# Block-sparse attention and a gated feed-forward layer on one core: loads, row numbers, queues and low parts of the first jobs

## The chip, the cores and the metric

One core of a Trainium2 chip. The metric is the device time of one execution in microseconds; the comparison is by the median of the runs.

## The reference, cut to what matters

```python
B, H, S, D = 4, 8, 768, 64            # block = 32, 24 blocks
scores = (q @ k.T) / sqrt(D)          # masked: neighbours, first and last block, 3 sampled blocks of each row of blocks
attn = softmax(scores); x = (attn @ v) as (B*S, H*D) = (3072, 512)
h = x @ w_in                          # 512 -> 2048, weights float64
g = h * tanh(log1p(exp(h)))
out = g @ w_out                       # 2048 -> 512
```

## The kernel before, in words

Every float32 operand of a product is cut into a high and a low float16 part, and each product is three matmuls (high-high, high-low, low-high). A low part is the scaled value less its high part; in the kernel before it is made by VectorE or GpSimd.

**Attention.** A batch is 13 jobs: blocks 0 and 23 are dense (all 768 keys), the other 22 blocks of queries go in pairs, called here the two halves of a job. A half has 256 keys: three neighbours, two global blocks, three sampled ones. `gather_k` (L537) copies the sampled keys inside SBUF on GpSimd (L544). `gather_v` (L551) fetches values from the DRAM copy `vd`, which `store_v` (L500) writes: one DMA for the neighbours (L560) and three for the sampled blocks (L567), all by SyncE's queue, each of the three after a load of its row number into a register (L528, from the table `offv`); of three numbers two stay in registers for later batches. There are two buffers of gathered keys and two of gathered values (L306); `globals_v` (L516) puts the global blocks there. A job then runs: scores `s` on TensorE (L604), maximum on VectorE (L647), exponentials on ScalarE (L670), transposes `t` on TensorE (L690), high part `ph` on ScalarE (L693), low part `pl` on VectorE (L697), product with values into `obank` (L719, for early jobs one half at a time), division `xs` on VectorE (L741), transposes `tx` (L748), high part `xh` (ScalarE, L766), low part `xl` (VectorE, L769). The PSUM ring `t` has two buffers and each is held from L690 until `pl` is made.

**Values, batch 0.** `load` (L368) puts q, k and v into the ring `raw` of six buffers. Tiles in `APART` (L498) are scaled in place on ScalarE or GpSimd (L466, L468), their high part is on ScalarE (L477) and their low part on GpSimd (L483); others take ScalarE (L448) and VectorE (L452).

**Weights.** They arrive as float64: 8 pieces of w_in (1 MB, ring `wr` of three) and 16 of w_out (0.5 MB, ring `raw`), loaded by SyncE's queue (L785). VectorE puts float32 together in three steps each (L793, L796, L799); TensorE, VectorE and ScalarE find a scale, and GpSimd makes the low parts (L857, L896).

**Feed-forward.** 12 tiles of 256 tokens. `moe_h` (L924) makes h (L935) and `moe_g` (L951) the gate in the ring `us` (L958 to L968) and two parts `g` (L976, L979, ring of four); `moe_y` (L982) multiplies by w_out (L994), one tile behind. Tile 0 needs the results of jobs 0 to 4.

**Order.** No loop sets the order. Every step is a task with an engine, an assumed duration, its inputs and outputs and a key; `Plan.emit` (L85) places tasks one after another by the assumed times, and a smaller key goes earlier. What is emitted is a fixed program for each engine. `START` (L1136) holds back a job's scores against other work of TensorE, and idle stretches of the plan between 14 and 200 us are filled with matmuls on zeros (L1173).

Of the kernel before, what the change touches and what calls it, by code (L numbers as in the profile page):

```python
# [26 lines left out]
             xs=2, hs=3, us=3, g=4, ys=1, kt=1, q=2, ssk=2, ssv=2, ssq=2, sck=2, scv=2, scq=2, iv=2, ns=3, ws=2,  # L27
# [13 lines left out]
class Plan:  # L41
# [43 lines left out]
    def emit(self, pace, fill):  # L85
# [6 lines left out]
        free, ready, dma = {}, {}, 0.0  # L92
# [10 lines left out]
        while todo:  # L103
# [35 lines left out]
            if port and free.get("POOL", 0.0) > start:  # L139
                t.dur *= 1.3  # L140
            end = start + t.dur + (pace(t, None) or 0.0)
            free[t.eng] = end
            if t.kind and t.kind[0] == "dma":

                dma = max(dma, end) + t.kind[1]
                t.end = max(dma, end + t.lat)
            else:
                t.end = end + t.lat
# [19 lines left out]
def attn_mish_kernel(ctx: ExitStack, tc: tile.TileContext, qT, kT, v, sampled, blocks, w_in, w_out, out):  # L168
# [45 lines left out]
    wo = const.tile([P, NFC, 2, DM], F16, name="wo")  # L214
    iv_i = const.tile([P, NFP], F32, name="iv_i")
    iv_o = const.tile([P, 1], F32, name="iv_o")
    sc_o = const.tile([P, 1], F32, name="sc_o")
    gsc = const.tile([P, NFP], F32, name="gsc")
    gmx = const.tile([P, 1], F32, name="gmx")
    iv_x = const.tile([P, B], F32, name="iv_x")  # L220
    iv_k = const.tile([P, B], F32, name="iv_k")
    gox = const.tile([P, 1], F32, name="gox")
# [19 lines left out]
    def which(new):  # L242
        room = new(sb, "raw", ("z",), [P, RAW])
# [47 lines left out]
    zeros = const.tile([P, NZ], F16, name="zeros")  # L291
    nc.gpsimd.memset(zeros, 0.0)
# [13 lines left out]
    NKG = NVG = 2  # L306
# [37 lines left out]
    def root_pe(key, ss, apart):  # L344

        n = ss.shape[-1]
        tp = new(ps["t"], "t", key, [P, n if apart else 1])
# [15 lines left out]
    def add_root(key, ss, fn, r, after, w, new, cls, n=1, apart=False):  # L363

        add("PE", 0.3 * n, lambda: root_pe(key, ss(), apart), r=r, w=[key], new=[("t", key)], key=cls - 2, lat=0.3)
        add("DVE", 0.6, fn, r=[key, *after], w=w, new=new, key=cls)

    def load(b, what, js, ring="raw", after=()):  # L368
# [3 lines left out]
        def fn():  # L372
            for j, key in zip(js, keys):
                raw = new(sb, ring, key, [P, RAW])[:, 0:4 * TT]
# [30 lines left out]
    def scales(b, what, j, cls):  # L405
# [4 lines left out]
        def fn():  # L410
# [5 lines left out]
            if q:  # L416

                ns = new(sb, "ns", ("ns", b, j), [P, 2])
                for n, sign in enumerate((1.0, -1.0)):
# [4 lines left out]
                 [(f"sc{what}", key)] + ([("ns", ("ns", b, j))] if q else []), cls, 1 if q or not b else NTT)  # L424
# [73 lines left out]
    APART = {("v", 0, 0), ("v", 0, 1), ("v", 0, 2), ("q", 0, 1), ("q", 0, 2), ("k", 1, 0), ("k", 1, 1), ("k", 1, 2)}  # L498
# [25 lines left out]
    def block_at(eng, name, table, k, hi):  # L524
# [4 lines left out]
        if k % NR < 2:  # L529
            regs[name, k] = j  # L530
        return j

# [4 lines left out]
    def gather_k(su):  # L537
# [3 lines left out]
        def fn():  # L541
            for k, c0 in slots(su):
                j = block_at(nc.gpsimd, "k", offk, k, S - BS)
                nc.gpsimd.tensor_copy(out=kgs[n][:, :, c0:c0 + BS], in_=tl["kt", b][:, :, ds(j, BS)])  # L544
# [676 lines left out]
```

## Time and profile before

| what | us |
|---|---|
| runs | 796.12, 790.94, 795.52; median 795.52 |
| the profiled execution | 792.27, its span 790.5 |
| TensorE busy in the span | 740.3 (94%) |
| VectorE, ScalarE, GpSimd busy | 523.3, 534.0, 350.2 |

The profile is of one execution. Busy time of TensorE counts filler matmuls, and matmuls are pipelined, so busy is not the same as full. A stretch table gives each engine's busy time between two moments; the queue of SyncE (SPq) shows DMA issues, not transfers.

### The profile page before, as it was taken

The page shows a single profiled execution, that of the slowest core. Times are in us where ns is not written, and L with a number is a line of the kernel's source. Part 1 is how long each engine was busy: PE and PEld are TensorE (multiplying, and loading weights), DVE is VectorE, ACT ScalarE, POOL GpSimd, SP SyncE. Part 2 cuts the span into 40 slices and gives each one's busy share as a digit, 9 for nine tenths or more (in the row PEclk, how much of TensorE's full clock was granted, in tenths as well). Part 3 has the DMA queues.
Part 4 walks back from the last instruction along what each step waited for, and adds up shares of the span by engine and source line. Part 5 has one row for each costly group of instructions (what it writes and reads, how often), then busy time and mean ns, then how long its engine had stood idle before and what let it go on. Part 6 is the DMA issues. An engine that isn't in the chain of part 4 may idle for free.

```text
span 790.5 us, 30717 instructions
## 1 busy us (share of the span) xinstructions
PE 740.3 (94%) x12857; PEld 528.6 (67%) x12857; DVE 523.3 (66%) x914; ACT 534.0 (68%) x831; POOL 350.2 (44%) x413
## 2 busy tenths in 40 slices
PE   5757769999999999999999999999999999999997
PEld 4646658766577667776777676667677676666653
DVE  5998888689977755669566766786867553323240
ACT  2565246788787857887877787867877774555550
POOL 2499442589953424425433643345444431303031
PEclk9958889999999999999999999999999999999999
DMA  8855867612424356326424454253343243000000
GB/s 285 283 170 160 246 192 210 171 54 64 128 95 133 87 154 195 88 89 191 117 68 116 135 166 132 68 172 103 82 115 105 76 134 84 15 14 14 14 14 27
DMA packets 56974, 94.25 MB, mean 119 GB/s; under 512 B 8067, under 2 KB 20356, under 8 KB 56836
## 3 DMA queue, kind: packets, MB, share of 16 engines
q1 hardware_dynamic: 56640, 92.03, 38.5%
q8 instruction: 101, 1.65, 0.9%
q14 instruction: 37, 0.30, 0.1%
q10 hardware_dynamic: 196, 0.27, 0.1%
HBM read 79.32 MB, written 12.95 MB: 117 GB/s over the span
## 4 chain that ended last, share of the span: by engine, by line
PE 75%; DVE 14%; DMA 4%; ACT 2%; issue 2%; POOL 2%; SPq 1%; POOLq 0%; ACTq 0%; DVEq 0%
PE y L994 28%; PE h L935 27%; PE t L690 6%; PE obank L719 5%; PE s L604 5%; PE obank L1173 2%; DVE wi L796 2%; DVE pl L697 1%; PE tx L748 1%; DVE mx L647 1%; DVE wi L799 1%; DVE hs L968 1%; DMA vg<-vd 1%; DVE us L962 1%; DVE q L452 1%
## 5 line engine op out<-in xcount | busy, mean ns | idle before, releaser
L935 PE MATMUL h<-xh,wi 128*128 128x256 f16 x1536 | 283.6, 273 | 0.0
L994 PE MATMUL y<-wo,g 128*128 128x512 f16 x1152 | 276.7, 379 | 3.0 <-POOL wo L896 1.4
L935 PEld LDWEIGHTS <-wi 128*128 128x128 f16 x2304 | 223.9, 98 | 51.0 <-issue 2.4
L935 PE MATMUL h<-xl,wi 128*128 128x256 f16 x768 | 210.0, 273 | 0.7 <-issue 0.7
L979 POOL TENSOR_TENSOR g<-hs,g 128x1024 f16<-128x1024 f32 x48 | 105.9, 2206 | 187.8 <-DVE g L976 158.1
L994 PEld LDWEIGHTS <-g 128*128 128x128 f16 x1152 | 110.4, 98 | 105.5 <-issue 6.2
L544 POOL COPY kg<-kt 128x256 f16 x264 | 118.3, 488 | 110.1 <-PE s L604 103.7
L944 ACT ACTIVATE hs<-h,gsc 128x512 f32<-128x512 f32 x96 | 65.5, 684 | 73.1 <-PE h L935 71.7
L670 ACT ACTIVATE pt<-s,nb,ns 128x256 f32<-128x256 f32 (+1 forms) x208 | 106.4, 582 | 6.6 <-DVE nb L660 3.4
L697 DVE SCALAR_TENSOR_TENSOR pl<-t,ph 128x512 f16<-128x512 f32 x112 | 75.6, 683 | 39.8 <-ACT ph L693 39.6
L693 ACT ACTIVATE ph<-t 128x512 f16<-128x512 f32 x112 | 65.5, 594 | 50.6 <-PE t L690 34.6
L968 DVE SCALAR_TENSOR_TENSOR hs<-us,hs 128x1024 f32<-128x1024 f32 x48 | 65.5, 1364 | 33.2 <-ACT us L967 33.2
L690 PE MATMUL t<-ident,pt 128*128 128x128 f32 x448 | 72.9, 287 | 6.8 <-DVE pl L697 4.8
L964 POOL TENSOR_TENSOR us<-us 128x1024 f32<-128x1024 f32 x21 | 40.9, 1949 | 74.6 <-DVE us L962 68.9
L962 DVE TENSOR_SCALAR us<-us 128x1024 f32<-128x1024 f32 x48 | 41.9, 872 | 39.4 <-ACT us L958 39.2
L719 PEld LDWEIGHTS <-ph 128*32 128x32 f16 x3584 | 49.0, 95 | 27.3 <-issue 18.8
L690 PEld LDWEIGHTS t<-ident,pt 128*128 128x128 f32 x448 | 52.9, 145 | 17.7 <-DVE pl L697 6.8
L647 DVE TENSOR_REDUCE mx<-s 128x4 f32<-128x1024 f32 x44 | 53.3, 1211 | 4.2 <-PE s L604 4.2
L958 ACT ACTIVATE us<-hs,hsc 128x1024 f32<-128x1024 f32 x48 | 55.2, 1151 | 1.0
L719 PE MATMUL obank<-vg,ph 128*32 128x65 f16 (+1 forms) x3072 | 49.2, 197 | 6.5 <-DMA vg<-vd 4.3
L966 ACT ACTIVATE us<-us 128x1024 f32<-128x1024 f32 x48 | 50.7, 1055 | 4.7 <-POOL us L964 4.1
L967 ACT ACTIVATE us<-us 128x1024 f32<-128x1024 f32 x48 | 50.7, 1056 | 0.7
(193 smaller groups left out, 945.9 us busy)
## 6 DMA issues: line engine op xcount, KB each, us to landing
vg<-vd SPq DMA_DIRECT2D x304, 65.0 KB, 2.4
vg<-vd SPq DMA_DIRECT2D x80, 195.0 KB, 2.9
wr<-in_moe_w_in_dram SPq DMA_DIRECT2D x8, 1024.0 KB, 6.7
wor<-in_moe_w_out_dram SPq DMA_DIRECT2D x16, 512.0 KB, 4.5
vd<-v SPq DMA_DIRECT2D x12, 520.0 KB, 3.6
raw_k<-in_k_dram SPq DMA_DIRECT2D x12, 512.0 KB, 4.9
raw_q<-in_q_dram SPq DMA_DIRECT2D x12, 512.0 KB, 4.2
raw_v<-in_v_dram SPq DMA_DIRECT2D x12, 512.0 KB, 6.0
```

Of the source, the lines that this page charges most:

```text
L544: nc.gpsimd.tensor_copy(out=kgs[n][:, :, c0:c0 + BS], in_=tl["kt", b][:, :, ds(j, BS)])
L647: nc.vector.tensor_reduce(out=mx.rearrange("p g w -> p (g w)"), in_=tl[ks].rearrange("p g (w k) -> p (g w) k", k=KT), axis=AX.X, op=ALU.max)
L670: ex = lambda o, x, g, w: nc.scalar.activation(out=o, in_=x, func=AF.Exp, bias=nb[:, g, w:w + 1], scale=tl["ns", b, sus[w]["qb"] // TB][:, ...
L690: nc.tensor.transpose(t[:, k, g], src, ident)
L693: nc.scalar.activation(out=new(sb, "ph", ("ph", i, j), [P, 2, 2, P], F16), in_=tl["t", i, j], func=AF.Copy, scale=PSC)
L697: nc.vector.scalar_tensor_tensor(out=new(sb, "pl", ("pl", i, j), [P, 2, 2, P], F16), in0=tl["t", i, j], scalar=PSC, in1=tl["ph", i, j], op ...
L719: nc.tensor.matmul(o[cs, w, g, 0:v1 - v0], p[:, k, g, cs], vt[:, k, 2 * c + g, v0:v1], start=j == 0 and g == 0 and k == 0 and n == 0, stop ...
L935: nc.tensor.matmul(h[:, f2].rearrange("p (s q) -> p s q", q=BS), wi[:, fp, w, cc, fs], x[:, :, cc], start=f2 == 0 and k == 0, stop=f2 == 1 ...
L944: nc.scalar.activation(out=tl[kq][:, 2 * (fp % 2):2 * (fp % 2) + 2], in_=tl[kh], func=AF.Copy, scale=gsc[:, fp:fp + 1])
L968: add("DVE", 1.32, lambda: nc.vector.scalar_tensor_tensor(out=hs(), in0=us(), scalar=-0.5, in1=hs(), op0=ALU.add, op1=ALU.mult), r=[ku], w ...
L979: add("POOL", 2.3, lambda: nc.gpsimd.tensor_tensor(out=g()[:, 1], in0=hs(), in1=g()[:, 0], op=ALU.subtract), r=[kq, ("gh", b, t, k)], w=[kg])
L994: nc.tensor.matmul(tl[ky], tl["g", b, t, k][:, g, f, q], wo[:, fc, w], start=fc == 0 and n == 0, stop=fc == NFC - 1 and n == 2)
```

## The change

The values of batch 0, and the first tile of q, are loaded into buffers of the rings `us` and `hs` instead of `raw`, and their parts are made by ScalarE and VectorE. The row numbers that stay in registers are loaded for batch 0 by SyncE as tasks of their own (`registers`). All loads of weights are issued by ScalarE's queue. There are three buffers of gathered values; the ring `us` has two instead of three. For jobs 0 to 6 (`APL`) and for the first piece of w_in (`LPE`) the low part is made so: TensorE adds the negative of the high part into the PSUM bank that holds the value (a matmul with a negative identity), and ScalarE reads the bank. The gathered keys of jobs 0 to 6 may be copied by ScalarE. Job 12 takes the neighbours of the keys out of the batch's own tile, in matmuls of their own, instead of copying them (`WHOLE`; job 13 is dense), and job 11's product with values is one task (`SPLIT`). The planner counts the DMA time of each queue apart and takes GpSimd 15% slower beside VectorE. The roots of batch 0's k and first q use the PSUM ring `y`. Keys, `START` and the moments of batch 1's loads differ.

```diff
-             ... us=3, g=4, ...
+             ... us=2, g=4, ...
...
             if port and free.get("POOL", 0.0) > start:
                 t.dur *= 1.3
+            elif t.eng == "POOL" and free.get("DVE", 0.0) > start:
+                t.dur *= 1.15
...
+    neg = const.tile([P, 2, P], F16, name="neg")
+    nc.vector.tensor_scalar(out=neg[:, 0], in0=ident, scalar1=-1.0, scalar2=None, op0=ALU.mult)
+    nc.vector.tensor_scalar(out=neg[:, 1], in0=ident, scalar1=-1.0 / PSC, scalar2=None, op0=ALU.mult)
...
-    NKG = NVG = 2
+    NKG, NVG = 2, 3
...
-    APART = {("v", 0, 0), ("v", 0, 1), ("v", 0, 2), ("q", 0, 1), ...
+    APART = {("q", 0, 1), ...
...
-        if k % NR < 2:
+        if stays(name, k):
             regs[name, k] = j
+    def stays(name, k):
+        return k % NR < 2
+    def registers(su):
+        for r in range(NR):
+            k = su["qb"] * NR + r
+            if stays("v", k):
+                add("SP", 0.75, lambda k=k: block_at(nc.sync, "v", offv, k, S), r=["off"], w=[("reg", k)], key=99)
...
+                if eng == "ACT":
+                    j = nc.scalar.value_load(offk[0:1, k:k + 1], min_val=0, max_val=S - BS)
+                    nc.scalar.activation(out=dst, in_=tl["kt", b][:, :, ds(j, BS)], func=AF.Copy)
...
+        add("POOL", 0.53 * NR, lambda: fn("POOL"), r=KT3(b) + ["off"], w=[("kg", n)], use=[("kt", b)], key=-3,
+            also=[("ACT", 0.55 * NR, lambda: fn("ACT"))] if su["early"] else ())
...
-    WHOLE = 12
-    SPLIT = 12
+    WHOLE = 14
+    SPLIT = 11
+    APL = 7
...
+        def td_fn(j):
+            nc.tensor.matmul(tl["t", i, j].rearrange("p k g q -> p (k g q)"), neg[:, 1],
+                             tl["ph", i, j].rearrange("p k g q -> p (k g q)"), start=False, stop=True,
+                             skip_group_check=True)
+        def plf_fn(j):
+            nc.scalar.activation(out=new(sb, "pl", ("pl", i, j), [P, 2, 2, P], F16), in_=tl["t", i, j], func=AF.Copy,
+                                 scale=PSC)
...
+            if i < APL:
+                add("PE", 0.23, lambda j=j: td_fn(j), r=[("ph", i, j)], w=[kj], key=-3, lat=0.25, kind=("T", i))
+                add("ACT", 0.62, lambda j=j: plf_fn(j), r=[kj], w=[("pl", i, j)], new=[("pl", ("pl", i, j))],
+                    key=-2.5)
+                continue
...
+            run(lambda x, hi, lo: nc.tensor.matmul(x, neg[:, 0], hi, start=False, stop=True, skip_group_check=True))
+            run(lambda x, hi, lo: nc.scalar.activation(out=lo, in_=x, func=AF.Copy))
...
+        if i < APL:
+            add("PE", 0.15, xd_fn, r=[("xhw", i)], w=[("tx", i)], use=kx, key=-3, lat=0.25, kind=("X", i))
+            add("ACT", 0.4, xlf_fn, r=[("tx", i)], w=[("xw", i)], use=kx, key=-1.5)
+        else:
+            add("DVE", 0.45, xl_fn, r=[("tx", i), ("xhw", i)], w=[("xw", i)], use=kx, key=-1.5)
...
-        nc.sync.dma_start(out=raw.rearrange(...) if len(w.shape) == 3 else raw, in_=w)
+        nc.scalar.dma_start(out=raw.rearrange(...) if len(w.shape) == 3 else raw, in_=w)
...
-            add("SP", 0.5, lambda: load_w(pools["w"], raw, "wr", src, None), w=[raw], new=[("wr", raw)], key=-2,
-                lat=2.0, kind=("dma", 4.4))
+            add("ACT", 0.45, lambda: load_w(pools["w"], raw, "wr", src, None), r=after, w=[raw], new=[("wr", raw)],
+                key=-9, lat=2.0, kind=("dma", 4.4))
...
+        if k >= LPE:
+            add("POOL", 2.1, lambda: nc.gpsimd.tensor_tensor(out=lo, in0=tl[kt], in1=hi, op=ALU.subtract),
+                r=[kt, ("wih", k)], w=[("wi", k)], key=cls)
+            return
+        for n in range(2):
...
+                nc.tensor.matmul(d, ident, tl[kt][:, cs], start=True, stop=False)
+                nc.tensor.matmul(d, neg[:, 0], hi[:, cs], start=False, stop=True)
+            add("ACT", 0.62, lambda kd=kd, cs=cs: nc.scalar.activation(out=lo[:, cs], in_=tl[kd], func=AF.Copy),
+                r=[kd], w=[("wl", k, n)], key=cls)
...
-        add("SP", 0.5, lambda: load_w(sb, raw, "raw", ...), r=after, w=[raw, ("wo", fc)], ..., key=0, ...)
+        add("ACT", 0.45, lambda: load_w(sb, raw, "raw", ...), r=after, w=[raw, ("wo", fc)], ..., key=-5, ...)
...
-    AT0, ATV, ATW = -16.0, -28.0, 2.0
+    LPE = 1
+    AT0, ATV, ATW = -15.0, -19.0, 1.0
...
-    load(0, "q", [0])
+    load(0, "q", [0], "hs")
     for j in T3:
-        load(0, "v", [j])
+        load(0, "v", [j], "us" if j < 2 else "hs")
...
+    for job in jobs[0:JB]:
+        for su in job["sus"]:
+            if not job["dense"]:
+                registers(su)
...
-            PREP = (6, 4, 3) if b else (8, 1, 8)
+            PREP = (6, 4, 3) if b else (8, 2, 7)
...
-            LOADO, ATO, ATP = [("dec", 6)], -1.0, -4.0
+            LOADO, ATO, ATP = [("dec", 6)], -1.0, -15.0
...
-    RES, START = 155.0, [0, 51, 57, 72, 69, 48, 81, 72, 9, 0, 0, 0, 0, 0]
+    RES, START = 155.0, [0, 66, 57, 72, 72, 57, 99, 72, 15, 12, 9, 24, 6, 18]
```

## Rows read from the trace of the kernel before

**Rows 1.** The page's first line, and its row of TensorE's busy tenths in 40 equal slices of the span.
```profile
span 790.5 us, 30717 instructions
...
PE   5757769999999999999999999999999999999997
```
**Rows 2.** Busy time of each engine in four stretches (us from the span's start, length, then busy us and number of instructions of PE, PEld, DVE, ACT, POOL, then the granted clock, the DMA engines' share and GB/s).
```profile
0.00:122.00 122.00, 83.34 (x1944) 67.25 (x1945) 103.72 (x196) 56.09 (x90) 72.10 (x88) 0.85 0.70 224
122.00:200.00 78.00, 73.27 (x1413) 57.44 (x1411) 64.94 (x104) 64.81 (x106) 52.51 (x41) 0.98 0.44 126
200.00:790.50 590.50, 583.67 (x9504) 403.92 (x9502) 354.67 (x616) 413.12 (x636) 225.54 (x286) 1.00 0.33 97
...
10.00:122.00 112.00, 79.62 (x1918) 64.31 (x1917) 99.90 (x175) 54.81 (x89) 70.14 (x79) 0.83 0.69 219
```
**Rows 3.** The first matmul of the feed-forward part in order of time, the row of all matmuls with w_out (duration min/median/max in ns, first and last start in us), the filler matmuls of the first 122 us by line and shape (busy us, mean ns), and the matmuls of L935 alone in two stretches (busy us and number on PE, then on PEld).
```profile
121.60 0.42 PE L935 MATMUL h<-xh,wi 128*128 128x256 f16 x1
...
L994 PE MATMUL y<-wo,g x1152: 376/379/391, 157.9 to 785.9; 128*128 128x512 f16 x192
...
L1173 PE MATMUL obank<-zeros 128*128 128x240 f16 x231 | 34.2, 302 | 5.7 <-DVE xs L741 5.4 <-issue 0.3
...
122.00:157.90 35.90, 24.30 (x192) 18.30 (x189) 0.95 0.66 183
157.90:200.00 42.10, 21.46 (x182) 17.29 (x180) 1.00 0.26 77
```
**Rows 4.** SyncE's queue in order of time (start us, length of the merged piece us, what).
```profile
13.39 0.91 SPq L381 DMA_DIRECT2D raw_v<-in_v_dram  x1
...
37.53 2.92 SPq L501 DMA_DIRECT2D vd<-v  x2
...
56.73 0.38 SPq L501 DMA_DIRECT2D vd<-v  x1
57.17 5.79 SPq L519 DMA_DIRECT2D vg<-vd  x4
63.01 0.63 SPq L560 DMA_DIRECT2D vg<-vd  x1
...
69.76 2.57 SPq L567 DMA_DIRECT2D vg<-vd  x3
```
**Rows 5.** The same queue by line, 60 to 122 us for the gathers: issue time min/median/max in ns, first and last start; then the time from issue to landing of L567, and the issues of w_out.
```profile
L560 SPq DMA_DIRECT2D vg<-vd x12: 323/380/632, 63.0 to 120.8; - x12
...
DMA to landing us min/median/max: 1.8/4.1/6.5
...
L785 SPq DMA_DIRECT2D wor<-in_moe_w_out_dram x16: 328/382/1040, 72.9 to 120.3; - x16
```
**Rows 6.** VectorE in order of time: the products xs of jobs 1 and 4.
```profile
79.33 0.42 DVE L741 TENSOR_TENSOR xs<-obank,r 128x256 f32<-128x256 f32 x1
...
110.71 0.42 DVE L741 TENSOR_TENSOR xs<-obank,r 128x256 f32<-128x256 f32 x1
```
**Rows 7.** VectorE, 0 to 122 us, by line and shape (number | busy us, mean ns | idle before), then single lines with min/median/max in ns.
```profile
L796 DVE SCALAR_TENSOR_TENSOR wi<-wr,wi 128x1024 int32<-128x1024 int32 x8 | 15.3, 1915 | 0.0
L799 DVE SCALAR_TENSOR_TENSOR wi<-wr,wi 128x1024 int32<-128x1024 int32 x8 | 11.8, 1474 | 0.0
L697 DVE SCALAR_TENSOR_TENSOR pl<-t,ph 128x512 f16<-128x512 f32 x16 | 10.8, 682 | 3.8 <-ACT ph L693 3.8
L796 DVE SCALAR_TENSOR_TENSOR wo<-wor,wo 128x512 int32<-128x512 int32 x11 | 10.6, 963 | 0.0
...
L452 DVE SCALAR_TENSOR_TENSOR q<-raw_q,sc_q,q 128x1024 f16<-128x1024 f32 x1 | 1.3, 1277 | 0.0
...
L769 DVE TENSOR_TENSOR xl<-tx,xh x6: 273/350/417, 62.9 to 116.8; 128x128 f16<-128x128 f32 x3, 128x256 f16<-128x256 f32 x3
...
L796 DVE SCALAR_TENSOR_TENSOR wi<-wr,wi x8: 1212/1314/3149, 22.3 to 68.0; 128x1024 int32<-128x1024 int32 x8
L799 DVE SCALAR_TENSOR_TENSOR wi<-wr,wi x8: 1210/1223/2939, 24.0 to 71.6; 128x1024 int32<-128x1024 int32 x8
...
L796 DVE SCALAR_TENSOR_TENSOR wo<-wor,wo x16: 678/683/2499, 80.3 to 134.6; 128x512 int32<-128x512 int32 x16
```
**Rows 8.** GpSimd, 0 to 122 us, by line and shape.
```profile
L544 POOL COPY kg<-kt 128x256 f16 x54 | 28.0, 548 | 15.1 <-PE s L604 11.1 <-POOL kg L544 2.2 <-issue 1.1
L857 POOL TENSOR_TENSOR wi<-wt_i,wi 128x1024 f16<-128x1024 f32 x8 | 19.7, 2472 | 4.0 <-ACT wi L854 3.9
L483 POOL TENSOR_TENSOR v<-raw_v,v 128x1024 f16<-128x1024 f32 x3 | 7.6, 2557 | 0.0
...
L468 POOL TENSOR_SCALAR raw_v<-raw_v,sc_v 128x1024 f32<-128x1024 f32 x1 | 2.1, 2074 | 11.2 <-DVE gram_wi L340 11.2
```
**Rows 9.** ScalarE, 0 to 122 us, by line and shape.
```profile
L693 ACT ACTIVATE ph<-t 128x512 f16<-128x512 f32 x17 | 10.1, 596 | 25.9 <-PE obank L719 13.5 <-PE t L690 12.3
...
L466 ACT ACTIVATE raw_v<-raw_v,sc_v 128x1024 f32<-128x1024 f32 x2 | 2.3, 1144 | 2.5 <-DVE sc_v L231 2.5
...
L766 ACT ACTIVATE xh<-tx 128x256 f16<-128x256 f32 x3 | 1.2, 386 | 2.1 <-PE tx L748 2.1
```
**Rows 10.** One of VectorE's lines of the feed-forward part over the whole run (min/median/max ns).
```profile
L968 DVE SCALAR_TENSOR_TENSOR hs<-us,hs x48: 1207/1224/3152, 141.7 to 768.9; 128x1024 f32<-128x1024 f32 x48
```
**Rows 11.** What the DMA engines moved in the first 130 us, and one stretch of 10 us (columns as in rows 2).
```profile
DMA packets 15440, 29.45 MB, mean 227 GB/s; under 512 B 1525, under 2 KB 5078, under 8 KB 15416
...
20.00:30.00 10.00, 9.01 (x129) 8.20 (x107) 9.62 (x15) 4.45 (x8) 0.92 (x3) 1.00 0.88 301
```
**Rows 12.** What SyncE's queue waited for in the first 200 us (us in total, times, longest).
```profile
SPq L785 <- DVE wi L799: 25.5, 5, 7.7
```

More of the change, by code (lines that the diff above doesn't have):

```diff
@@ L91, in emit @@
                 d.then.append(t)
-        free, ready, dma = {}, {}, 0.0
+        free, ready, dma = {}, {}, {}
         def open_(t):
@@ L342, in add_gram, with root_pe @@
         add("DVE", 0.4, diag, r=[kg], w=w, new=new_, key=cls - 2)
-    def root_pe(key, ss, apart):
+    def root_pe(key, ss, apart, ring):
         n = ss.shape[-1]
-        tp = new(ps["t"], "t", key, [P, n if apart else 1])
+        tp = new(ps[ring], ring, key, [P, n if apart else 1])
         if apart:
@@ L373, in fn @@
             for j, key in zip(js, keys):
-                raw = new(sb, ring, key, [P, RAW])[:, 0:4 * TT]
+                raw = new(sb, ring, key, [P, RAW]) if ring == "raw" else \
+                    new(sb, ring, key, [P, 4, TT]).rearrange("p f q -> p (f q)")
+                raw = raw[:, 0:4 * TT]
                 if what == "v":
@@ L423, in scales @@
         add_root(kp, lambda: tl[ks][:, 0:1] if q or not b else tl[ks], fn, [ks], [("sc", "k", b, 0)] if q else [], [key] + ([("ns", b, j)] if q else []),
-                 [(f"sc{what}", key)] + ([("ns", ("ns", b, j))] if q else []), cls, 1 if q or not b else NTT)
+                 [(f"sc{what}", key)] + ([("ns", ("ns", b, j))] if q else []), cls, 1 if q or not b else NTT,
+                 ring="t" if b or j else "y")
     def parts(b, what, j, cls):
@@ L567, in fn @@
                 nc.sync.dma_start(out=vg[p0:p0 + BS, c0 // P], in_=vd[b][ds(j, BS)])
-        add("SP", 2.9, fn, r=VD3(b) + ["off", "z"], w=[("vg", n)], key=-3, lat=2.4, kind=("dma", 0.9))
+        add("SP", 2.9, fn, r=VD3(b) + ["off", "z"] + [("reg", k) for k, _ in slots(su)], w=[("vg", n)], key=-3, lat=2.4,
+            kind=("dma", 0.9))
     def fetch_dense(su):
@@ L607, in scores, with transpose @@
                             stop=last and n == len(PROD) - 1 and m == len(pieces) - 1)
+    def transpose(out, src, start, stop):
+        nc.tensor.matmul(out, src, ident, start=start, stop=stop, is_transpose=True)
     def attend(job):
@@ L780, in load_w @@
         if not wide:
-            nc.sync.dma_start(out=a0, in_=w)
+            nc.scalar.dma_start(out=a0, in_=w)
             return
@@ L1033, in attn_mish_kernel @@
             su["whole"] = job["i"] >= WHOLE
+            su["early"] = job["i"] < APL
     wpool_cm = tc.tile_pool(name="wraw", bufs=2)
@@ L1172, in fill @@
         for _ in range(n):
-            nc.tensor.matmul(obank[:, NO:NO + NZ], zeros[:, 0:P], zeros, start=True, stop=True)
+            nc.tensor.matmul(obank[:, NO:NO + NZ], neg[:, 0], neg.rearrange("p n q -> p (n q)")[:, 0:NZ],
+                             start=True, stop=True)
         return max(n, 0)
```

66 lines of the change are left out of this document (35 added, 31 removed).

## The prediction

> **What bounds the kernel now.** I read the page's row of TensorE in 40 slices first, then a table of stages, then the queues and engines of the first stage. The row of slices shows TensorE at nine tenths from about the ninth slice on [rows 1]. The stage table says it in numbers: from 200 us to the end TensorE is busy 583.67 of 590.5 us, while in the first 122 us it is busy 83.34, so 38.7 us are idle there [rows 2], and 34.2 of the busy time are matmuls on zeros [rows 3]. The first matmul of the feed-forward part starts at 121.6 us and the first one with w_out at 157.9 [rows 3]. Behind 121.6 it idles 4.7 of 78 us, then hardly at all [rows 2]. So the time of this kernel is a head of about 122 us, with at most 49 us of needed work on TensorE in it (83.34 less 34.2), and a full stretch behind it. What moves the first feed-forward matmul moves the end, as long as TensorE stays fed behind it.
>
> What sets 121.6? Two chains run through the head. The first is the gathered values. The third v tile is issued only at 13.39, the last of the three stores of values at 56.73, and the first gather follows at 63.01 [rows 4]. Then 12 halves of jobs are gathered between 63.0 and 120.8 [rows 5]: 57.8 over 11 is 5.25 us for a half, 10.5 for a job. The division xs of job 1 is at 79.33, that of job 4 at 110.71 [rows 6]: 10.46 us a job. The two agree: SyncE's gathers set the pace of the jobs, and 11 us after job 4's division the feed-forward part starts. The second chain is VectorE, busy 99.9 of the 112 us from 10 to 122 us, 89% [rows 2]: it decodes the weights, and w_out is needed at 157.9.
>
> **The change part by part.** All sums are made against the profiled execution, 792.27 us with a span of 790.5; the median of the runs is 795.52, or 3.25 higher, and I put half of that, 1.6, on the result.
>
> Values early. The loads no longer wait for a free buffer, so all seven tiles are issued in one go instead of the last at 13.39. The scale then comes some 9 us earlier at least, say at 20 us (an estimate), and three tiles of 1.277 us on VectorE [rows 7] end at about 25. The last store lies between that and 37.5, where the first was before [rows 4]; I take 30, 27 us earlier than 56.73. The first gather moves from 63 to about 36.
>
> Row numbers and third buffer. Three issues of L567 with their loads take 2.57 us, so 1.12 from one to the next, of which the issue is 0.33 [rows 4]. With two of three numbers in registers a half takes 0.38 + 1.12 + 2 x 0.33 = 2.2 us of SyncE's queue [rows 4, 5]. The loads moved ahead are 44 of about 0.8 us, 35 us of SyncE; from 8 us on the queue has little else, the weights having left it, and each gather needs only its own two, so I cost them at nothing; if the first gather had to wait for all, it would stay near 43. A buffer is taken for 2.2 + 4.1 us of landing [rows 5] and the product; over three buffers that is 2.1 us a half and a little, over two 3.2. Either way the gathers fall from 10.5 to about 5 us a job and no longer set the pace.
>
> What is late next is ScalarE. From 10 to 122 us it is busy 54.8 [rows 2]. Added: low parts pl of jobs 0 to 4, 11 tiles at the 0.596 of ph [rows 9], 6.6; xl of five jobs at 0.386, 1.9; the issues of 24 weight loads at 0.382 [rows 5], 9.2; the low part of w_in's first piece, two halves at 0.596, 1.2. The copies of gathered keys on ScalarE aren't in the trace: between none and all 36 of jobs 1 to 6, at the 0.386 of xh as the nearest row [rows 9], so 0 to 13.9; I take a third, 4.6, because GpSimd is the first choice and often free. Taken off: two tiles of v scaled at 1.144, 2.3. The sum is 54.8 + 6.6 + 1.9 + 9.2 + 1.2 + 4.6 - 2.3 = 76.0 us. ScalarE's own share in the full stretch from 122 to 200 is 64.81 of 78, 83% [rows 2]; 76.0 at 83% is 91.6 us, so the feed-forward part starts at 101.6, **20 us earlier**. With no key copies it is 25.6, with all 8.8.
>
> VectorE. Off: 15 tiles of pl at 0.682, 10.2, and six xl at 0.35, 2.1; on: three low parts of v at 1.277, 3.8, and two small ones for the negative identity, about 0.3 [rows 7]. Decoding runs slower than its least duration: 8 x (1.915 - 1.212) + 8 x (1.474 - 1.210) + 11 x (0.963 - 0.678) = 10.8 us [rows 7], beside a GpSimd busy 70.1 us [rows 2]. GpSimd loses 7.6 + 2.1 of v, 2.5 of w_in and a third of 36 copies at 0.548, 6.6: 18.8 or 27% [rows 8], so 2.9 of the 10.8. VectorE comes to 88.8 from 99.9; 11.1 less at 89% is 12.5 us. So w_out is ready 12.5 us earlier, less than the 20. The gap of 7.5 is covered: h of tile 1, 21.5 us of matmuls, ran after 157.9 [rows 3] and can run ahead of w_out.
>
> TensorE gets 15 matmuls of 512 columns and some short ones. L994's 0.379 [rows 3] bounds them above, 5.7 us; below they cost nothing, since 38.7 idle and 34.2 filler microseconds lie there. I take nothing; without the cover it is 5.7. They add a wait: the correction waits for ph, and behind it on TensorE stand the next scores, the weights' scales and fillers, for which VectorE's maximum waits; 15 x 0.596 = 9 us at most, in the same idle time, and the wait for VectorE's pl goes in exchange. That also frees the ring t without VectorE.
>
> The rest I cost at nothing. The ring us of two: 48 gates in 627 us, one in 13 us, and a gate is six operations mostly near 1.2 [rows 10], 7 to 10 us, so two suffice. Job 12's keys and job 11's product: a few tenths at most on TensorE. Keys, START and the planner's factors only reorder. Issuing weights elsewhere leaves the bytes as they are.
>
> Sum: 792.3 - 20 + 1.6 = **774**.
>
> **The rivals.** *VectorE still sets the head* (786 to 788). The low parts of v now stand on VectorE with two inputs from memory while GpSimd copies keys; the same form takes 1.207 alone and up to 3.152 at worst [rows 10]. Three at 3.15 add 5.6 us, VectorE falls only 5.5, 6.2 at 89%: 792.3 - 6.2 + 1.6 = 787.7. For it: VectorE's 89%. Against: only w_out, not tile 0, needs the whole stream. The Trainium skill, "SBUF — State Buffer", section "SBUF: two separate sides", has a VectorE operation with two inputs there and a reading GpSimd operation exclude each other for a whole instruction; the spread of row 10 agrees.
>
> *The transfers set it* (782). The first 130 us move 29.45 MB at a mean of 227 GB/s, and 301 was reached for 10 us [rows 11]. At 250, a tenth above the mean, the same bytes take 118 us: 12 us earlier, 792.3 - 12 + 1.6. For it: weights now compete with gathers instead of standing in line with them. Against: 301 would allow 98 us. The Trainium skill, "DMA: Bandwidth & Descriptors", section "Issuing engines are not separate DMA queues", says that another issuing engine saves only issue time; no run here shows it yet.
>
> *Attention runs free* (760). Without ScalarE as a limit, job 1's product is at 36 + 6.3 = 42, job 4's three jobs of 8 us later, and the start at 77. Then w_out limits: 12.5 us, and at most the 21.5 of tile 1's h done ahead: 34 gained. Against it: 83% of ScalarE.
>
> *ScalarE stands behind the weights* (805, slower). SyncE waited 25.5 us in five waits for VectorE to free a buffer of w_in [rows 12], and had nothing else to do. If ScalarE takes these waits over, in front of its exponentials, 76.0 + 25.5 = 101.5 at 83% is 122.3: the start is at 132.3, 10.7 later. It decides from waits of some 16 us on. Against: the plan places the loads where it believes the buffer free, and ScalarE's later arrival shortens the waits.
>
> *The plan undoes it* (792): other orders in the head cost what the parts gain.
>
> **How the numbers follow.** Forecast 0.46, VectorE 0.14, transfers 0.10, free attention 0.14, ScalarE 0.12, undone 0.04. The forecast's own range is 764 to 784, from the bounds of the key copies (25.6 and 8.8). From free attention with a little below it to the undone plan the range is 757 to 793; it leaves out most of the slower case. A difference of about 1%, 788 or 803 here, is what a measurement of this kernel can tell from no change. Faster: 0.45 + 0.07 + 0.08 + 0.14 = 0.74. Slower: two thirds of the ScalarE case, 0.08. The rest, 0.18, is within 1%.
>
> **What would show it.** Right: the first matmul of L935 near 100 us; the last store of values near 30; gathers some 5 us a job when they run; VectorE's 0 to 122 us without pl of jobs 0 to 6; TensorE full behind the start; the first w_out matmul near 145. Wrong: an unmoved start with ScalarE's queue at L785 in front of its idle time, decoding at over 2 us a step, or a gap of TensorE behind the start, waiting for w_out.

## Result: 0.9% slower, with the first feed-forward matmul 22 us earlier

The changed kernel takes 801.59 us (median of 17 runs, 797.27 to 807.41), the kernel before 794.20 (17 runs, 790.52 to 797.89): a ratio of 1.0093 with an interval of 1.0069 to 1.0117. The forecast was 774. The profiled execution of the changed kernel took 797.3 us with a span of 795.5, near the low end of its runs; it stands against 792.27 and 790.5 of before.

The page of the changed kernel, its first line and TensorE's busy tenths, and the stages as in [rows 1, 2]:
```profile
span 795.5 us, 30849 instructions
...
PE   6677787699999999999999999998999999999997
```
```profile
0.00:122.00 122.00, 88.83 (x2265) 69.31 (x2265) 99.83 (x188) 68.96 (x132) 63.53 (x75) 0.93 0.78 242
122.00:200.00 78.00, 65.89 (x1026) 48.71 (x1030) 71.24 (x102) 61.28 (x94) 47.03 (x41) 0.98 0.37 113
200.00:795.50 595.50, 583.99 (x9610) 406.11 (x9609) 351.55 (x616) 413.83 (x634) 226.60 (x278) 1.00 0.33 96
```
Compare the stages. In the first 122 us TensorE is busy 5.5 us more than before, from 122 to 200 it is busy 7.4 us less. Without the filler matmuls (19.8 and 6.7 us of these stretches here, 34.2 and none before) it does 20 us more of needed work in the first and 14 us less in the second. Behind 200 us it does the same work, 583.99 against 583.67, in 595.5 us against 590.5: it idles 11.5 us there, where it idled 6.8.

The answers to [rows 3]: the first matmul of the feed-forward part, the row of all with w_out (min/median/max ns, first and last start), the matmuls of h alone in four stretches (busy us and number on PE, then PEld):
```profile
99.62 0.27 PE L1001 MATMUL h<-xh,wi 128*128 128x256 f16 x1
...
L1060 PE MATMUL y<-wo,g x1152: 376/379/390, 160.2 to 791.2; 128*128 128x512 f16 x192
...
99.60:121.60 22.00, 13.27 (x108) 10.19 (x108) 1.00 0.74 216
121.60:137.00 15.40, 9.88 (x84) 8.05 (x84) 1.00 0.48 145
137.00:157.00 20.00, 0.11 (x2) 0.07 (x1) 0.91 0.52 167
157.00:200.00 43.00, 17.04 (x144) 13.95 (x144) 1.00 0.26 77
```
The first is 22 us earlier (99.6 for 121.6), the second 2.3 us later (160.2 for 157.9). And there is a hole: tile 0's 192 matmuls are done at 137, and from 137 to 157 h stands still. Before, 192 of them ran in 122 to 157.9 without a hole [rows 3]. Counted by their weight loads, with a matmul of y (the product with w_out) as two of h, because it has twice the columns, the changed kernel has 101 done at 120 us where before had none, 192 against 83 at 137, and 216 against 212 at 160 (before: 192 of h and 10 of y). Of the lead 4 are left at 160 us.

SyncE's queue as in [rows 4], and VectorE's quotients xs of jobs 1, 4 and 8 as in [rows 6]:
```profile
25.02 3.50 SPq L506 DMA_DIRECT2D vd<-v  x3
34.02 4.40 SPq L524 DMA_DIRECT2D vg<-vd  x6
39.03 0.63 SPq L581 DMA_DIRECT2D vg<-vd  x1
```
```profile
60.23 0.42 DVE L781 TENSOR_TENSOR xs<-obank,r 128x256 f32<-128x256 f32 x1
...
86.28 0.42 DVE L781 TENSOR_TENSOR xs<-obank,r 128x256 f32<-128x256 f32 x1
...
148.61 0.42 DVE L781 TENSOR_TENSOR xs<-obank,r 128x256 f32<-128x256 f32 x1
```
Job 1 is 19 us earlier, job 4 24 us, job 8, which tile 1 needs, only 2 us (150.64 before). Between jobs 4 and 8 the changed kernel takes 62 us, the one before 40. VectorE, the third engine in these rows, is full while tile 1 is missing (columns as in [rows 2]):
```profile
130.00:140.00 10.00, 7.67 (x115) 6.17 (x112) 10.00 (x13) 7.52 (x12) 3.49 (x2) 1.00 0.24 61
...
137.00:157.00 20.00, 12.74 (x233) 10.23 (x231) 19.05 (x32) 14.86 (x22) 9.28 (x5) 0.91 0.52 167
```
VectorE's decode of w_out, by line (number | busy us, mean ns), in the changed kernel and then in the one before, each up to its own end:
```profile
L849 DVE SCALAR_TENSOR_TENSOR wo<-wor,wo 128x512 int32<-128x512 int32 x16 | 17.1, 1082 | 0.0
L846 DVE SCALAR_TENSOR_TENSOR wo<-wor,wo 128x512 int32<-128x512 int32 x16 | 16.3, 1028 | 0.0
L843 DVE TENSOR_SCALAR wo<-wor 128x512 int32<-128x512 int32 x16 | 13.2, 835 | 3.8 <-DMA wor<-in_moe_w_out_dram 3.7
```
```profile
L796 DVE SCALAR_TENSOR_TENSOR wo<-wor,wo 128x512 int32<-128x512 int32 x16 | 14.3, 899 | 0.0
L799 DVE SCALAR_TENSOR_TENSOR wo<-wor,wo 128x512 int32<-128x512 int32 x16 | 12.4, 787 | 0.0
L793 DVE TENSOR_SCALAR wo<-wor 128x512 int32<-128x512 int32 x16 | 8.5, 543 | 0.2 <-DMA wor<-in_moe_w_out_dram 0.2
```
The same 48 instructions take 46.6 us in place of 35.2, and the last ends at 144.9 where it ended at 138.3. Two places of the timeline show how, first on GpSimd, then on VectorE (start us, length us):
```profile
117.48 2.13 POOL L910 TENSOR_TENSOR wi<-wt_i,wi 128x1024 f16<-128x1024 f32 x1
119.57 2.07 POOL L1030 TENSOR_TENSOR us<-us 128x1024 f32<-128x1024 f32 x1
...
137.39 2.13 POOL L1045 TENSOR_TENSOR g<-hs,g 128x1024 f16<-128x1024 f32 x1 [6.03 <-DVE wo L849]
```
```profile
117.78 4.15 DVE L843 TENSOR_SCALAR wo<-wor 128x512 int32<-128x512 int32 x2
...
136.05 0.68 DVE L846 SCALAR_TENSOR_TENSOR wo<-wor,wo 128x512 int32<-128x512 int32 x1
...
137.59 2.48 DVE L846 SCALAR_TENSOR_TENSOR wo<-wor,wo 128x512 int32<-128x512 int32 x1
```
L846 takes 0.68 with GpSimd idle (the one at 136.05); started 0.2 us into a low part of g it ends 0.55 us after it. From 100 us to the end of the decode GpSimd is busy 27.2 of 44.9 us, before 13.8 of 38.3: the earlier gates, the last pieces of w_in and the keys of jobs 5 to 8 now stand beside the decode.

Behind 200 us the waits of TensorE (us in total, times, longest) begin with a releaser that the list of before doesn't have there:
```profile
PE obank L759 <- issue: 2.9, 3, 1.6
PE s L627 <- issue: 2.4, 2, 1.6
```
In such a stretch TensorE waits for nothing that the profile shows. There are five of over 0.5 us, in the middle of runs of matmuls of one kind. Two of them, then what the DMA engines moved in the last half microsecond before 554 and in the stretch around the first of the two:
```profile
556.71 0.52 PE L627 MATMUL s<-kg,q 64*32 64x256 f16 x24 [1.60 <-issue]
...
656.00 0.21 PE L759 MATMUL obank<-vg,ph 128*32 128x64 f16 x2 [1.65 <-issue]
```
```profile
q8 instruction: 1, 0.02, 17.7%
...
DMA packets 0, 0.00 MB, mean 0 GB/s; under 512 B 0, under 2 KB 0, under 8 KB 0
```
From 551 to 557 us that packet, in flight from 553.98 to 555.40, is the only transfer, so this one is neither a wait for data nor contention with other transfers. What comes ahead of each of the five is one packet of the queue named instruction, at 344.1, 393.5, 504.8, 554.0 and 653.1; the gaps end at 346.3, 395.9, 507.1, 556.7 and 656.0, 2.2 to 2.9 us later. The page has 101 such packets with 1.65 MB, 16 KB each. The trace has 12,896 weight loads and as many matmuls on TensorE; 25,792 by 101 is 255, so 128 matmuls with their loads make about one packet.

The traces show whose packets these are. Number TensorE's instructions by their starts: matmuls, weight loads and the few of its sequencer. In the 18 traces of this document all 162 stops of over 0.2 us without a releaser end at the same place of 256, number 193 or 194 counted from 0. TensorE passes such a place 1,806 times in them, and never sooner than 2.16 us after the start of the packet that belongs to it (the first packet to the first such place behind number 256, and so on). So TensorE waits there for its own instructions. The changed kernel has seven such stops ahead of 200 us as well, 8.6 us in all, the longest 2.4 us at 124.4; the kernel before has three there, 3.2 us in all.

### The profile page after: what moved, and what is told of

Read it like the earlier page. It is cut to its first block, busy times and chain, and to the rows that moved or that the text cites. A ratio compares the mean times of both kernels' runs of the same rounds, so it can differ in the third digit from the quotient of the medians.

```text
span 795.5 us, 30849 instructions
## 1 busy us (share of the span) xinstructions
PE 738.7 (93%) x12896; PEld 524.1 (66%) x12896; DVE 522.6 (66%) x904; ACT 544.1 (68%) x859; POOL 337.2 (42%) x392
## 3 DMA queue, kind: packets, MB, share of 16 engines
q8 instruction: 101, 1.65, 0.9%
## 4 chain that ended last, share of the span: by engine, by line
PE 74%; DVE 11%; DMA 7%; issue 3%; ACT 3%; SPq 2%; POOL 1%; ACTq 0%; DVEq 0%; POOLq 0%
PE y L1060 28%; PE h L1001 26%; PE obank L759 6%; PE t L633 6%; PE s L627 4%; DMA raw_q<-in_q_dram 2%; PE obank L1247 1%; PE tx L633 1%; DVE wo L846 1%; DVE wo L849 1%; DVE wt L957 1%; SPq L588 1%; DVE wo L843 1%; DMA vg<-vd 1%; DMA wr<-in_moe_w_in_dram 1%
## 5 line engine op out<-in xcount | busy, mean ns | idle before, releaser
L1045 POOL TENSOR_TENSOR g<-hs,g 128x1024 f16<-128x1024 f32 x48 | 109.9, 2290 | 222.5 <-DVE g L1042 186.7
L724 DVE SCALAR_TENSOR_TENSOR pl<-t,ph 128x512 f16<-128x512 f32 x97 | 66.2, 684 | 43.7 <-ACT ph L720 43.6
L1034 DVE SCALAR_TENSOR_TENSOR hs<-us,hs 128x1024 f32<-128x1024 f32 x48 | 63.7, 1328 | 28.4 <-ACT us L1033 27.9
L633 PE MATMUL t<-ident,pt 128*128 128x128 f32 x448 | 70.5, 281 | 4.7 <-ACT pl L733 2.4
L1028 DVE TENSOR_SCALAR us<-us 128x1024 f32<-128x1024 f32 x48 | 39.3, 819 | 44.9 <-ACT us L1024 44.9
L1030 POOL TENSOR_TENSOR us<-us 128x1024 f32<-128x1024 f32 x18 | 36.3, 2018 | 47.3 <-DVE us L1028 41.7
L1032 ACT ACTIVATE us<-us 128x1024 f32<-128x1024 f32 x48 | 50.7, 1055 | 3.0 <-POOL us L1030 2.1
L627 PEld LDWEIGHTS <-q 64*32 64x32 f16 x3024 | 33.7, 92 | 28.6 <-issue 24.9
```

The costliest lines, as they stand in the source:

```text
L627: nc.tensor.matmul(s[g][i * BS:(i + 1) * BS, c0 + cs.start:c0 + cs.stop], q[gs, c * NPR + i, qs], src[gs, a * NPR + i, ks], start=first an ...
L633: nc.tensor.matmul(out, src, ident, start=start, stop=stop, is_transpose=True)
L724: nc.vector.scalar_tensor_tensor(out=new(sb, "pl", ("pl", i, j), [P, 2, 2, P], F16), in0=tl["t", i, j], scalar=PSC, in1=tl["ph", i, j], op ...
L1034: add("DVE", 1.32, lambda: nc.vector.scalar_tensor_tensor(out=hs(), in0=us(), scalar=-0.5, in1=hs(), op0=ALU.add, op1=ALU.mult), r=[ku], w ...
L1045: add("POOL", 2.3, lambda: nc.gpsimd.tensor_tensor(out=g()[:, 1], in0=hs(), in1=g()[:, 0], op=ALU.subtract), r=[kq, ("gh", b, t, k)], w=[kg])
```

## Experiments

Medians are in us; a ratio stands against runs of the kernel before on the same chip at the same time, with its interval.

**One part undone at a time.** Two buffers of values, three of us; the weights back on SyncE's queue; no low parts on TensorE and no key copies on ScalarE; the planner's transfers on one clock.
```
NKG, NVG = 2, 2      RINGS us=3      globals_v per half                   (u_buf)
nc.sync.dma_start(...) in load_w, add("SP", ..., key=-2 / 0)              (u_queue)
APL = 0      LPE = 0                                                      (u_low)
dma["all"] = max(dma.get("all", 0.0), end) + t.kind[1]                    (u_dma)
```


> The changed kernel with two buffers of gathered values and three of the gate's ring, as before; all else as changed. Three theories. Decode theory (w_out is decoded no earlier, because GpSimd's work stands beside VectorE's once the feed-forward part starts early): this edit leaves the head, first w_in matmul near 100, first w_out matmul near 160, time 797 to 803. Transfer theory (weights on ScalarE's queue delay the small transfers): the same, 797 to 803. Late theory (the buffers cost what TensorE idles after 200 us, 11.5 against 6.8 us of idle time): TensorE idles about 7 us after 200, time 792 to 796.

> The changed kernel with all weight loads issued by SyncE's queue again. Transfer theory: the second q tile lands sooner, TensorE's wait for it at 20 us (6.5 us) is gone, decoding of w_out ends 6 us or more sooner than at 145, time 790 to 795. Decode theory: decoding ends within 3 us of 145 and the time stays at 797 to 803, or worse where gathers stand behind weights again. Late theory: 797 to 803.

> The changed kernel with no low parts made on TensorE (jobs 0 to 6 and the first piece of w_in on VectorE and GpSimd as before) and no key copies on ScalarE. Decode theory: VectorE gets 10 us of pl back and GpSimd its copies, so decoding ends later than 145 by 5 to 10 us, time 803 to 812. Transfer theory and late theory: the low parts don't matter for the loss, within 3 us of the changed kernel.

> The changed kernel, but the planner counts the DMA time of all queues together again, as before; the program is only ordered otherwise. Transfer theory: the plan knows the second q tile to be late and puts other work ahead of it on TensorE, the 6.5 us wait is gone, time 790 to 796. Decode theory: first w_out matmul within 5 us of 160, time 797 to 803. Late theory: 797 to 803.


Measured: 805.6 (1.0134, 1.0096 to 1.0172), 802.1 (1.0114, 1.0059 to 1.0170), 803.7 (1.0111, 1.0085 to 1.0137), 806.5 (1.0157, 1.0133 to 1.0181). No part alone carries the loss. The late theory falls: u_buf idles 13.3 us behind 200, not 7. The transfer theory falls: the wait of 6.5 us is gone in u_queue and in u_dma, u_queue's decode ends at 124.2, and neither is faster. The decode theory fits u_low alone, whose decode ends at 155.7: u_queue's decode and u_dma's first y come earlier than it allows, and u_buf's first y (169.3) and time later. u_queue has the first y at 136.1 and u_dma at 144.0, both far earlier than 160.2, and neither gains by it, for h of tile 1 starts at 169.4 and 168.5 there in place of 157.0; TensorE's idle behind 200 us is 11.6 to 17.0 us in all four.

**The numbers of the order.** The old ones back (u_order), the old WHOLE and SPLIT alone (u_split), the decode of w_out behind the attention (p_ato).
```
START, AT0, ATV, ATW, ATP, PREP, WHOLE, SPLIT of before                   (u_order)
WHOLE = 12    SPLIT = 12                                                  (u_split)
ATO = 12.0                                                                (p_ato)
```


> The changed kernel with the order numbers of the kernel before: earliest starts of the jobs, keys of the early pieces and of w_out's parts, point of the next batch's preparation, WHOLE and SPLIT. Theory 3 (the new numbers hold jobs 4 to 8 back, above all job 6 at 99 us where it was 81): xs of job 8 before 140 and a time of 788-796. Rival (the numbers follow the resources and are worth little): 799-808.

> The changed kernel with WHOLE and SPLIT of the kernel before (12 and 12 in place of 14 and 11): jobs 12 and 13 read their scores in one piece, job 11's product with the values is issued in two steps. It also shifts the program behind job 12 by some 100 instructions. Theory 4 (gaps by position): the gaps after 200 us change places and their sum changes; the time is within 797-806. Theory 5 (the two numbers cost by themselves): 794-798 with the head unchanged.

> The changed kernel with the key of the w_out decode set from -1 to +12, so that on VectorE the attention of jobs 4 to 8 and the gates go ahead of the decode. Theory 2 (job 8's rows, which tile 1 needs, come late because VectorE decodes w_out first; TensorE's hole at 137-157 is that): xs of job 8 comes at 130-140 in place of 148.6, tile 1's h starts there, the hole closes, the first y moves to 160-168, and the time falls to 786-795. Rival (VectorE is full in any order, so what h gains y loses): 798-806.


Measured: 814.9 (1.0255, 1.0220 to 1.0290), 797.8 (1.0064, 1.0033 to 1.0094), 810.8 (1.0207, 1.0146 to 1.0267). Theory 3 falls: with the old numbers job 8's quotient is at 177.6. Theory 2 falls too: in p_ato it came at 134.3, as expected, but the decode ended at 159.9 and the first y was at 170.2. u_split's time lies in the ranges of both its theories; its gaps behind 200 us are 2.3 us in place of 5.9, as theory 4 expects, and its head is not unchanged, as theory 5 wants it (the first h is at 104.1).

**GpSimd out of the decode's way.** First by leaving work out (n_pool), then by moving it, with a new plan (gate_act; tile 0 has four gates of 128x1024, not eight).
```
ps_ = slice(0, 8) if st == (0, 0) else slice(0, TT)    # columns of L1030, L1045   (n_pool)
st == (0, 0): square by nc.scalar, g's low part by nc.vector                       (gate_act)
```


> The changed kernel, every instruction in its place, but for tile 0's gates GpSimd squares and subtracts only 8 of 256 columns of each row (left out: the rest of the square and of g's low part, in whose place TensorE reads the high part). It takes some 13 us of GpSimd's work out of 119 to 158 us, beside the w_out decode. Theory 1 (VectorE waits for GpSimd at the memory and so sets the end of the head): w_out decode busy from 47-49 us to 36-40, its end from 145 to 134-138, job 8's xs from 148.6 to 138-143, and the time from 801.6 to 789-795. Rival (the end of the head hangs on something else, for example the order of the jobs): the decode gets shorter but the time stays within 798-804.

> The changed kernel with tile 0's eight gates off GpSimd: the square always by ScalarE, g's low part by VectorE (1.2 us each by the planner). Nothing is left out. Theory 1 (GpSimd's gate instructions hold VectorE up during the w_out decode): VectorE gains about 2 us per GpSimd instruction that it doesn't meet and pays 1.2 us per low part, ScalarE has room; w_out decode busy 38-43, job 8's xs 140-146, time 793-799. Rival (the order that the planner makes is shifted and the loss comes back elsewhere): 799-806.


n_pool: 792.8 (0.9983, 0.9948 to 1.0018), 8.8 below the changed kernel; its profiled run, 786.45, is the fastest of ten. Its decode, up to 138.5:
```profile
L849 DVE SCALAR_TENSOR_TENSOR wo<-wor,wo 128x512 int32<-128x512 int32 x16 | 14.2, 897 | 0.0
L846 DVE SCALAR_TENSOR_TENSOR wo<-wor,wo 128x512 int32<-128x512 int32 x16 | 13.9, 880 | 0.0
L843 DVE TENSOR_SCALAR wo<-wor 128x512 int32<-128x512 int32 x16 | 10.9, 694 | 3.1 <-DMA wor<-in_moe_w_out_dram 3.0
```
39.0 us for 46.6, job 8's quotient at 141.3 and tile 1's h at 149.8 for 157.0. Theory 1 held: the gate work of tile 0 stands in the way of tile 1. gate_act: 806.3 (1.0155, 1.0106 to 1.0204), with 39.7 us of decode; the rival held, at its upper end. Its TensorE had 7.9 us of stretches without a releaser behind 200 us, which the next runs explain.

**Is it the order or the run? The kernel before once more.**


> The kernel before once more, for a second profile of it. Question: in the changed kernel and all four kernels with one part undone TensorE stands still for 4.6 to 11 us after 200 us in stretches with no releaser ('issue'), in the middle of runs of short matmuls; the first profile of the kernel before had none of these after 200 us. Theory A (the gaps belong to the changed order): this second profile has under 1 us of them after 200 us. Theory B (they fall by chance, in any kernel): 3 us or more.


Measured: 793.2 in one run, and no such stretch behind 200 us, again, as theory A expects. In n_pool all five were back at the same runs of matmuls (starting at 336, 386, 497, 545 and 644 us, in a kernel that was some 10 us ahead): a property of the program.

**A shift of TensorE's program.** Small matmuls at the very front, where TensorE waits for k; nothing else is touched. 64 in the changed kernel (pad), 128 (pad128), 96 (pad96), and 64 in the kernel before (b_pad).
```
+    for _ in range(64):
+        nc.tensor.matmul(obank[:, NO:NO + 8], neg[:, 0], neg[:, 0, 0:8], start=True, stop=True)
     plan.emit(pace, fill)
```


> The changed kernel with 64 added matmuls of 8 columns at the very front of TensorE's program, where TensorE waits for the first rows of k; nothing else is moved. It shifts every later instruction of TensorE by 128 places (64 weight loads and 64 matmuls). Theory 4 (the stretches without a releaser are waits for TensorE's own instructions, of which a packet is fetched some 2.3 to 3.0 us before each gap ends; they fall where the end of a packet meets a run of short matmuls, so they hang on the position in the program): the gaps after 200 us, five with 5.7 us, turn up at other runs of matmuls or vanish, and the time goes by what is left of them, 796-804. Rival (they are a matter of the run itself, as of transfers at that time): the same five places as before, 5 to 6 us.

> The changed kernel with 128 small matmuls ahead of TensorE's program in place of 64: the shift is 256 places, which at 101 packets for some 25,900 instructions is one whole packet. Theory 4 (position within the fetched packets): the five gaps after 200 us of the changed kernel are back at the same runs of matmuls, 4.5 to 6.5 us in all, and the time is 797-806 like the changed kernel's. Rival (the 64 matmuls helped in another way, as by the clock at the start or by chance): gaps under 2 us and 790-796 like the kernel with 64.

> The changed kernel with 96 small matmuls in front of TensorE's program (a shift of three quarters of a packet). Theory 4: what the shift is worth goes with the position, so that 96 lies between 64 (792.7) and 128 (800.0): gaps after 200 us between 0.5 and 6 us, at fewer or other places than the five, and a time within 790-800. Rival (any shift helps but a whole packet): under 1 us of gaps and 791-794.

> The kernel before with 64 small matmuls of 8 columns at the front of TensorE's program. Theory 4: the kernel before has no gaps after 200 us only because its runs of short matmuls lie well in the packets; shifted by half a packet it gets 3 to 8 us of them and takes 797-803. Rival (the gaps belong to the changed kernel): none, 793-796.


Measured: pad 792.7 (0.9986, 0.9955 to 1.0018), pad128 800.0 (1.0065, 1.0043 to 1.0087), pad96 802.8 (1.0112, 1.0065 to 1.0158), b_pad 808.1 (1.0173, 1.0156 to 1.0190). The waits without a releaser behind 200 us, of pad, then three of the gaps of pad128, then of b_pad from 70 to 200 us:
```profile
PE obank L759 <- issue: 0.5, 1, 0.5
...
PE h L1001 <- issue: 0.2, 1, 0.2
```
```profile
349.95 0.30 PE L627 MATMUL s<-kg,q 64*32 64x256 f16 x8 [1.35 <-issue]
...
559.79 0.41 PE L627 MATMUL s<-kg,q 64*32 64x256 f16 x16 [1.05 <-issue]
...
658.33 0.21 PE L759 MATMUL obank<-vg,ph 128*32 128x64 f16 x2 [1.15 <-issue]
```
```profile
PE s L604 <- issue: 3.5, 1, 3.5
PE h L935 <- issue: 2.7, 1, 2.7
PE obank L719 <- issue: 1.1, 1, 1.1
```
Theory 4 held three times in the gaps; its times were missed twice, for pad came out under its range (796 to 804) and b_pad above (797 to 803). Half a packet takes the gaps away (0.7 us left) and 8.9 us off the time; a whole packet brings them back at the same five runs (5.7 us) and the time with them. In pad128 a packet again starts 2.2 to 2.5 us before these five gaps end. In pad the same run of a dense job's product, transposes and scores passes at 345 to 347.7 us without a stop: place 194 comes at 345.9, and its packet had started at 341.7. Ahead of 200 us pad has more of these stops than the changed kernel, 11.9 us for 8.6, so what the shift gave lies behind 200. The kernel before, shifted by half a packet, loses 13 us: 3.3 us of gaps behind 200 and 7.3 in the head for 3.2, where jobs come later (job 8's quotient at 159.2 for 150.6). 96 came out like 128, not between it and 64, with 4.3 us of gaps: here too the stops end at place 193 or 194, but in front of other matmuls, four of the five in front of h.

**Both together, and the order of x.** pad with tile 0's gates off GpSimd in the same planned order (swap_pad), and that with the steps from quotient to x first (x_first).
```
sq_fn: nc.scalar.activation(..., AF.Square) / lo_eng = nc.vector, for st == (0, 0)   (swap_pad)
key=-12 if i < 12 else -1.5   on xs, xh and xl                                       (x_first)
```


> The changed kernel with 64 small matmuls in front, and tile 0's four gates off GpSimd in the same planned order (the square by ScalarE, g's low part by VectorE, each in the place where GpSimd's instruction was issued). Nothing is left out. Theory 1 and theory 4 together: the shift alone gave 792.7; of the 8 us that leaving GpSimd's gate work out was worth, the low parts by VectorE (4 of some 1.2 us) and the waits in the planned order give some back: 786-791, w_out decode busy 38-43. Rival (what GpSimd did costs as much on VectorE and ScalarE): 791-796.

> As the kernel with 64 matmuls in front and tile 0's gates off GpSimd, and the keys of the steps from a job's sum to its x (quotient, high part, low part of the first 12 jobs) put ahead of all else on VectorE and ScalarE (-12 in place of -1.5). Theory 6 (tile 1's h waits for low parts of x that stand on VectorE behind gate work in the planned order; from job 8's quotient at 145.1 to h at 157-159): h of tile 1 starts 3 to 6 us sooner, and the time is 786-791. Rival (the plan as a whole shifts, and with it TensorE's program against the packets): 792-803.


Measured: swap_pad 793.7 (0.9965, 0.9934 to 0.9995), x_first 805.9 (1.0141, 1.0095 to 1.0187). swap_pad decodes in 39.3 us where pad needs 46.3, and is no faster than pad: the rival held. VectorE's order in it shows why:
```profile
145.09 0.42 DVE L781 TENSOR_TENSOR xs<-obank,r 128x256 f32<-128x256 f32 x1
...
154.23 2.17 DVE L1051 TENSOR_TENSOR g<-hs,g 128x1024 f16<-128x1024 f32 x1
156.33 0.47 DVE L809 TENSOR_TENSOR xl<-tx,xh 128x128 f16<-128x128 f32 x2
```
The quotient of job 8 is earlier, but its low part stands behind the gate's, and h of tile 1 starts at 157.2. Putting x first made another plan, with job 8's quotient at 160.7; that run doesn't decide theory 6.

## Why the prediction was wrong

The forecast was 774, 27.7 us too low. Of these, 20 are the earlier start, of which next to nothing was left by 160 us. Another 5.0 are what the profiled run took more than the one before, and 2.7 come from the runs' spread: the changed kernel's profiled run was 4.3 us under its median, where I had put 1.6.

*Values early, gathers no longer the pace*: right, with the stores at 25.0 (30 forecast), the first gather at 39.0 (36) and job 4's quotient 24 us earlier. Jobs 1 to 4 follow each other at 8.7 us where they took 10.5 (8 forecast).

*ScalarE is late next, the start at 101.6*: 99.6 measured, but not for the reason given, so the match is luck. From 10 to 99.6 us ScalarE is busy 52.3 of 89.6, and with the 16 issues of weights in that time, 6.2 us that don't count as busy, 65%; I had it at 83%. The keys' copies took 6.2 (4.6 taken). What sets 99.6 was not settled. The issues of weights held ScalarE's queue up twice, 2.6 and 2.4 us, and not for the 25.5 of the rival. The forecast's own range was also added up wrongly: 792.3 + 1.6 less 25.6 and 8.8 is 768 to 785, not 764 to 784.

*VectorE's 11.1 us less work brings w_out 12.5 us earlier*: wrong by 19 us; the decode ended 6.6 us later. VectorE's total fell, 99.90 to 95.70 from 10 to 122 us, though by 4.2 and not 11.1. I scaled the decode's slowdown by GpSimd's share of the first 122 us and let it fall by 2.9 us. But it goes by what GpSimd does at the same time: everything that came earlier, tile 0's gates first, moved into the w_out decode, which slowed by 11.4 us. The decode of w_in, which stands ahead of the gates, fell from 33.3 to 28.1 us. The rival with VectorE had the mechanism, but at the low parts of v, which took 1.28 us each and not 3.15. The Trainium skill, "SBUF — State Buffer", section "SBUF: two separate sides", says that a VectorE operation with two inputs in SBUF and a GpSimd operation that reads SBUF exclude each other for a whole instruction; the pair at 137.4 and 137.6 us agrees.

*The gap is covered by tile 1's h*: wrong. It needs job 8, and job 8 came 2 us earlier, not 20, because VectorE was full (100% from 130 to 140) with decode and gates. So TensorE's 109 matmuls of lead at 137 us were lost to the hole from 137 to 157. Here the argument failed as a whole: I moved the end of the head by the start of tile 0, while the head ends where tile 1 and w_out are there, and these hung on VectorE's whole work. n_pool shows the hang; how much of it is exclusion and how much the place of the gates in the order stays open, since swap_pad shortened the decode and gained nothing. What the stop of 2.4 us at 124.4 adds to job 8's delay was not tested.

*TensorE's added matmuls cost nothing*: up to 122 us they are 10 us (L728 5.7, the first piece of w_in 2.9, x 1.7), where my upper bound was 5.7 because it priced L728 alone, in idle time; giving them up in u_low brought nothing.

*TensorE stays full behind the start*: wrong by the gaps, and this makes the loss against the kernel before. With the lead gone at 160 us the two kernels stand nearly level, and behind 200 us the changed one idles 4.7 us more, 5.9 us being stretches without a releaser. The shift by 64 matmuls is worth 8.9 us in the medians, more than the whole loss of 7.4; the two profiled runs differ by 4.2 and their gaps behind 200 us by 5.2, and the rest may be the run-to-run spread, the changed kernel's profiled run being 4.3 us under its median. That TensorE waits for its own instructions is shown by the one place of 256 at which every stop ends. A run stops where it reaches that place less than 2.2 to 2.9 us after its packet started; what decides when a packet starts was not found.

*The rivals.* "The plan undoes it" (792) was nearest, without its cause. "Attention runs free" put job 1's product at 42 and the start at 77; job 1's quotient came at 60.2 and the start at 99.6. The transfers: moving the weights back to SyncE's queue changes nothing that can be measured (u_queue 802.1, 801.6 before it). The Trainium skill, "DMA: Bandwidth & Descriptors", section "Issuing engines are not separate DMA queues", says that another issuing engine saves only issue time; u_queue agrees. Ring us of two: giving back the third buffer, with the second of values, brought no gain either.

So the change itself is hidden under where each program happens to lie, and what it is worth alone stays open. At a shift of 0 the changed kernel is 7.4 us slower; with 64 matmuls in front of both it is 15.4 us faster (792.7 against 808.1, in two sets of runs in which the kernel before took 794.5 and 794.8), and with 96 or 128 in front it is back at 802.8 and 800.0; the kernel before was not run with these. Nothing tried was clearly faster than the kernel before as it is; the best ratio, swap_pad's, has an upper bound of 0.9995.

## What to carry to other kernels

Follow a gain past the first instruction that it moves: list what the next tile and the next stage need and on which engine each of them ends, and price an engine's slowdown by what stands beside it in the new order, not by its total. If TensorE stops in the middle of a run of short matmuls with no releaser, look for a packet of the instruction queue some 2 to 3 us earlier, count whether the stops lie a multiple of 256 instructions apart, and time the kernel with a few dozen idle matmuls in front before any other edit is judged. A difference of 1% between two kernels with long programs can be that alone.

## What was not expected of the hardware

- TensorE stood still 0.6 to 1.65 us at a time in five runs of short matmuls, each stop ending 2.2 to 2.9 us after the start of a 16 KB packet of the instruction queue, with 0 data packets in one of them; a shift by 64 matmuls took 5.2 of 5.9 us away, one by 128 gave them back.
- All 162 such stops of the 18 traces end at instruction 193 or 194 of 256; none of 1,806 passages of that place came sooner than 2.16 us after its packet.
- The same shift cost the kernel before 13.3 us (808.1 for 794.8).
- A VectorE instruction of 0.68 us took 2.48 when started 0.2 us into a 2.13 us GpSimd subtraction; two of 0.41 took 4.15 together beside a GpSimd square of 2.07 and the instruction ahead of it.
